# Talking-heads attention with a mixture of experts: the second head of each pair is placed through GpSimd's DMA queue, and the opening is re-ordered

## The chip, the core and the metric

The kernel runs on one core of a Trainium2 chip. A core has five engines that run their own instruction streams: TensorE (PE, with its weight loads shown apart as PEld), VectorE (DVE), ScalarE (ACT), GpSimd (POOL) and SyncE (SP). SP, ACT and POOL can issue DMA transfers, which 16 DMA engines carry out. The metric is the device time of one execution in microseconds (us). Before the change it was 724.6 us, the median of 3 runs (724.17 to 724.93).

## The reference

Twelve heads of attention over 4 batches of 448 tokens, with scores mixed across heads before the softmax (w_pre) and weights mixed across heads after it (w_post); then every token goes to the expert with the highest cosine similarity.

```python
scores = scale * np.matmul(q, k.transpose(0, 1, 3, 2))
scores = np.einsum('bhij,hg->bgij', scores, w_pre)
scores = scores - np.max(scores, axis=-1, keepdims=True)
attn = np.exp(scores)
attn = attn / (np.sum(attn, axis=-1, keepdims=True) + 1e-09)
attn = np.einsum('bhij,hg->bgij', attn, w_post)
x = np.matmul(attn, v)                 # then (4*448, 768)
logits = xn @ en.T / tau               # x and expert_emb normalised
expert_idx = np.argmax(logits, axis=1)
h = np.maximum(x[mask] @ w1[e], 0.0)   # for each of 8 experts
out[mask] = gate_w[mask, None] * (h @ w2[e])
```

## The kernel before, in words

The queries are cut into 16 tiles, four to a batch, of 120 rows (90 in the last tile of a batch; batch 0 begins with its 90-row tile). A tile has six pairs of heads. For each pair PE computes the scores (`emit_qk`, L259) into PSUM; DVE or ACT evicts them to a tile `s` of SBUF (`evict`, L263 to L269; six buffers of `s`); and `place` (L271 to L274) sends each of the two heads of the pair, by a DMA from SBUF to SBUF, into the group layout `g`, where 10 query rows of 12 heads share the partitions. One piece moves 120 (or 90) rows of 448 floats into 10 partitions: 210 or 157.5 KB. There are 96 pairs and so 192 pieces. Three group buffers `gb` serve the tiles in turn; they are called g_133, g_134 and g_135 in the rows of the program order, and tile 0 uses g_135. Their first four partitions are zeroed once.

A tile is then worked off in steps of two blocks of 10 query rows (92 steps in all). For a step, `emit_pre` (L294) multiplies `g` with w_pre on PE, `emit_max` (L302, DVE) and `emit_exp` (L311, ACT) make the softmax numerators `e` and their sums, `emit_r` takes the reciprocal (L319, L321, DVE) and lets POOL scale w_post with it (`wr`, L322), and `emit_post` (L337, L342) multiplies `e` with `wr` on PE. So the chain of a step is pre, max, exp, r, wr, post. In step s the program emits the score matmuls of a later pair, pre of step s+2, wr of step s+1, post of step s, and the placing of a pair as soon as the program order lets its group buffer be free (`held`, `free`). After post come the products with v, the routing, and from step 83 on the loads of the expert weights. The experts' part runs until the end.

The engines run in program order, so what stands ahead in an engine's stream delays what stands behind it. A tile framework adds the semaphore waits. Two of them matter here: a piece waits for the eviction of its `s` (and for the last reader of the group buffer), and every DMA counts on one of a few semaphores taken in turn, eight for the DMAs of SP and ACT together and eight for those of POOL, so that it waits until the DMA that used its semaphore before has landed.

The opening, before the steps begin (L794 to L832), computes 11 pairs (i = 0 to 10). SP loads q and k; POOL loads the small constants and zeroes two of the group buffers (L803); DVE zeroes the third (L799). PE fills its time with matmuls on a tile of ones (`warm`, L808). At i = 9 PE takes up `emit_pre(0)`, which reads the six pairs of tile 0. In the opening the second head of pairs 0 to 5 is sent by ACT, the first head by SP; from pair 6 on both are sent by SP.

Of the kernel before, what the change touches and what calls it, by code (L numbers as in the profile page):

```python
# [33 lines left out]
NPAIR = H // 2  # L34
# [12 lines left out]
def talking_heads_moe(  # L47
# [81 lines left out]
    with tc.manual_schedule():  # L129
# [36 lines left out]
        def embed():  # L166

            em = x_p.tile([128, DM], F32, tag="xs", name="em")[:E]
            ej = x_p.tile([128, DM], F16, tag="xj", name="ej")[:E]
            es = sm.tile([E, 1], F32, tag="es", name="es", bufs=1)  # L170
            G_.dma_start(out=em, in_=emb)
            G_.dma_start(out=wpre_sb, in_=wpre)
            A.activation(out=ej, in_=em, func=ACTF.Square, accum_out=es)
            A.activation(out=wpre_sb, in_=wpre_sb, func=ACTF.Copy, scale=0.125)
            yield
            G_.dma_start(out=rtau, in_=tau.to_broadcast([128, 1]))
            G_.dma_start(out=id_sb, in_=ident)
            G_.dma_start(out=valid_sb, in_=valid)
            G_.dma_start(out=tokid_sb, in_=tokid)
            G_.dma_start(out=tri_sb, in_=tri)  # L180
            yield
            V.tensor_scalar(out=ioE_b, in0=ioE, scalar1=-float(E), scalar2=None, op0=ALU.add)
            yield
            en_n = yield from newton_norm(sm, es, 1, "n1")
            V.tensor_scalar(out=en_n, in0=en_n, scalar1=1e-6, scalar2=None, op0=ALU.add)
            yield
            V.reciprocal(out=en_n, in_=en_n)
            yield
            G_.tensor_scalar(out=em, in0=em, scalar1=en_n[:, 0:1], scalar2=None, op0=ALU.mult)
            G_.tensor_copy(out=ien[:, :, :128], in_=id_sb.unsqueeze(1).to_broadcast([128, KD, 128]))  # L190
            for _ in range(5):
                yield
            p = ps_x.tile([128, 512], F32, tag="x", name="p_e")
            for kk in range(KD):
                T.transpose(p[:, kk * E:(kk + 1) * E], em[:, kk * 128:(kk + 1) * 128], id_sb[:E, :E])
            yield
            V.tensor_copy(out=ien[:, :, 128:], in_=p[:, :KD * E].rearrange("p (k e) -> p k e", e=E))
            V.reciprocal(out=rtau, in_=rtau)
            yield
            V.tensor_scalar(out=tie, in0=rtau, scalar1=-1.0, scalar2=None, op0=ALU.mult)  # L200
            yield
            V.tensor_tensor(out=tie, in0=tie, in1=rtau, op=ALU.max)
            yield
            V.tensor_scalar(out=tie, in0=tie, scalar1=2.0 ** -23, scalar2=None, op0=ALU.mult)
            V.tensor_tensor(out=tv, in0=tokid_sb, in1=valid_sb, op=ALU.mult)
            yield
            V.tensor_scalar(out=ioE_v, in0=ioE_b.unsqueeze(1).to_broadcast([128, NTL, E]), scalar1=-1.0, scalar2=None,
                            op0=ALU.add)
            yield
            V.tensor_tensor(out=ioE_v, in0=ioE_v, in1=valid_sb.unsqueeze(2).to_broadcast([128, NTL, E]), op=ALU.mult)  # L210
            yield
            V.tensor_scalar(out=ioE_v, in0=ioE_v, scalar1=1.0, scalar2=None, op0=ALU.add)
# [34 lines left out]
        def group(t):  # L247

            return gb[which[t]]

        def emit_qk(i, eng, pre=False):

            t, a = divmod(i, NPAIR)
            n = SZ[t]
            pq = ps_q.tile([128, 2, 512], F32, tag="q", name="p_q") if not pre else None
            p = [pq[:, r] for r in range(2)] if pq is not None else [ps_p.tile([128, 512], F32, tag="p", name="p_q") for _ in range(2)]
            for r in range(2):
                for w in range(2):
                    T.matmul(p[r][64 * w:64 * w + 64, :S], q_sb[t][64 * r:64 * r + 64, a, w, :],  # L259
                             k_sb[t // 4, a][64 * r:64 * r + 64], start=True, stop=True)  # L260

            def evict():
                sb = s_p.tile([128, 2, S], F32, tag="s", name="s")  # L263
                split = pq is None
                for o, i in [(sb[:, r], p[r][:, :S]) for r in range(2)] if split else [(sb, pq[:, :, :S])]:
                    if eng is A:
                        A.activation(out=o, in_=i, func=ACTF.Copy)  # L267
                    else:
                        V.tensor_copy(out=o, in_=i)  # L269

                def place(second=Y):  # L271
                    for r in range(2):
                        h = 4 + 2 * a + r
                        (second if r else Y).dma_start(out=group(t)[h:h + 109:12, :n // 10].rearrange("p c s -> p (c s)"), in_=sb[:n, r])  # L274
                return place
            return evict

# [433 lines left out]
        def bg_at(p, f):  # L711
            bg.setdefault(p, []).append(f)
# [84 lines left out]
        ge = embed()  # L797
        next(ge)
        V.memset(gb[2][:4], 0.0)  # L799
        consts()  # L800
        next(ge)
        for g in gb[:2]:
            G_.memset(g[:4], 0.0)  # L803
        p_w = ps_a.tile([128, 512], F32, tag="a", name="p_w")

        def warm(n):
# [3 lines left out]
        pend = []  # L810
        for i in range(N0):
            if i == 9:
                emit_pre(0, ps_m)
            if i == 10:
                emit_pre(1, ps_q)
            pend.append(emit_qk(i, A if i in (0, 8, 10) else V, i % 2 == 1 or i >= 10))
            if i < 9:
                warm(1)
            if i:
                pend.pop(0)()(A if i <= NPAIR else Y)  # L820
            if i == 8:
                load_q(2)
            if i == 9:
                emit_max(0)
                emit_exp(0)
        pend.pop()()()
        emit_max(1)
        emit_exp(1)
        for a in range(NPAIR):
            bg_at(1 + a, lambda a=a: load_v(0, a))  # L830
        warm(4)
        run(emit_r(0))  # L832
        qk_n = N0
        held = []
        placed = N0
# [6 lines left out]
        for s in range(ns):  # L842
            cr = emit_r(s + 1) if s + 1 < ns else iter(())
            evs = []
            ev = emit_post(s) if s == 0 else None
            want = due(s)
            assert want - qk_n < 3
            if qk_n < want:
                evs.append(emit_qk(qk_n, A))
                qk_n += 1  # L850
            if s + LEAD < ns:
                emit_pre(s + LEAD)
            if evict:
                evict()
            while tops:
                tops.pop(0)()
            next(cr, None)
            if evs:
                held.append(evs.pop()())
            while held and free(placed) <= s:  # L860
                held.pop(0)()
                placed += 1
            if s == ns - 2:
                px.close()
                pools["h"] = ctx.enter_context(tc.tile_pool(name="ps_h", bufs=2, space=PSUM))
                st_a = ffn_tok(first_rows["t"], w1p[0], w2p[0], first_rows["g"], idx_s[:, 0:1])
                steps_of(st_a, 1)
            if s == ns - 1:
                steps_of(st_a, 0)
            evict = ev or emit_post(s)  # L870
            next(cr, None)
            if qk_n < want:
                evs.append(emit_qk(qk_n, A))
                qk_n += 1
            for f in acts.pop(s, ()):
                f()
            if s + LEAD < ns:
                emit_max(s + LEAD)
                emit_exp(s + LEAD)
            if evs:  # L880
                held.append(evs.pop()())
                while held and free(placed) <= s:
                    held.pop(0)()
                    placed += 1
            for f in pes.pop(s, ()):
                f()
            for f in dves.pop(s, ()):
                f()
            for x in avs.pop(s, ()):
                emit_av(*x)  # L890
            for f in bg.pop(s, ()):
                f()
            if 3 <= s < 16:
                for _ in range(5):
                    next(ge, None)
            now[0] = s
            if s == first[NE + 1] + 3:
                gens += [(early(), 2), (gate_value(re, 0, NE, bank, routed_bank), 2)]
            if s == OPEN + 1:
                gens += [(first_x(), 1)]  # L900
            if s == first[NG + 1] + 1:
                gens += [(mid(), 2)]
            for g, n in gens:
                for _ in range(n):
                    next(g, None)
# [349 lines left out]
```

## Time and profile before

| | us |
|---|---|
| median of 3 runs | 724.6 |
| the profiled execution | 720.91 |
| its span on the core | 719.1 |
| PE busy | 684.0 |
| DVE busy | 462.0 |
| ACT busy | 393.4 |
| POOL busy | 117.8 |

Busy time is the time in which an engine executes an instruction; matmuls are pipelined, so a busy PE is not PE at its peak. "PEclk" is the share of the full clock (2.4 GHz) that was granted to PE, 0.50 being 1.2 GHz. "DMA" is the mean busy share of the 16 DMA engines. The releaser behind an arrow is what ended the idle time of an engine; "issue" means that the profile shows nothing that was waited for. SPq, ACTq and POOLq are the instruction queues of engines, where DMA issues appear.

### The profile page before, as it was taken

Reading aid. Unit: us, or ns where it says so; the run is one execution under the profiler, and the core shown is the slowest. Engines: PE = TensorE matmul, PEld = TensorE weight load, DVE = VectorE, ACT = ScalarE, POOL = GpSimd, SP = SyncE. Lnnn points to the kernel's source line nnn. Section 1 sums busy time; section 2 is a strip of 40 time slices with the busy share of each in tenths; the row PEclk is TensorE's granted clock in tenths of the full one; section 3 lists DMA queues with packets and bytes.
Section 4 is the critical chain, followed back from the end, with each engine's and each line's share of the span. In section 5 each row is a group of like instructions: output and inputs, shape, how many; then the busy total and the mean of one; then the engine's idle time right before and its main releaser. Section 6 shows DMA issues by size and latency. Waiting matters only on the chain. (4 is left out here: it accounts for less than half of the span.)

```text
span 719.1 us, 26009 instructions
## 1 busy us (share of the span) xinstructions
PE 684.0 (95%) x11132; PEld 560.5 (78%) x11132; DVE 462.0 (64%) x1069; ACT 393.4 (55%) x774; POOL 117.8 (16%) x179
## 2 busy tenths in 40 slices
PE   8788999999999989999999899999999999999983
PEld 4356767766677767676767689999999999999973
DVE  6476666666657656778657656868665656565661
ACT  2455666667567666666666644535263535453540
POOL 7020110110011101110120212330304040200000
PEclk9899999999999999999999999999999999999997
DMA  7676654776457754565343664776767676665750
GB/s 216 194 215 177 183 155 126 228 203 175 130 152 223 201 159 136 153 207 155 98 157 116 187 229 160 262 230 210 227 208 231 209 245 214 195 215 179 224 205 15
DMA packets 56709, 133.08 MB, mean 185 GB/s; under 512 B 6661, under 2 KB 31509, under 8 KB 56592
## 3 DMA queue, kind: packets, MB, share of 16 engines
q1 hardware_dynamic: 52472, 117.98, 53.2%
q0 software_dynamic: 3520, 12.44, 5.1%
q8 instruction: 89, 1.46, 0.8%
q10 hardware_dynamic: 600, 0.97, 0.4%
q14 instruction: 28, 0.23, 0.1%
HBM read 81.64 MB, written 12.20 MB: 130 GB/s over the span
## 5 line engine op out<-in xcount | busy, mean ns | idle before, releaser
L302 DVE TENSOR_REDUCE mn<-p_p 128x1 f32<-128x448 f32 (+1 forms) x182 | 105.6, 619 | 100.3 <-PE p_p L294 99.7
L580 ACT ACTIVATE wh<-raw_w 128x768 fp32r<-128x768 f32 (+2 forms) x132 | 114.9, 903 | 44.8 <-DMA raw_w<-w 39.4
L267 ACT ACTIVATE s<-p_q 128x896 f32<-128x896 f32 (+1 forms) x89 | 80.8, 908 | 104.3 <-PE p_q L259 94.2
L581 DVE TENSOR_TENSOR wl<-raw_w,wh 128x768 fp32r<-128x768 f32 (+2 forms) x132 | 130.9, 1026 | 9.3 <-ACT wh L580 8.8
L311 ACT ACTIVATE e<-p_p,mn 128x448 f32<-128x448 f32 (+1 forms) x182 | 113.6, 628 | 30.1 <-DVE mn L302 26.0
L337 PEld LDWEIGHTS p_m<-wr,e 64*64 64x64 f32 x4320 | 93.8, 135 | 44.4 <-issue 40.7
L337 PE MATMUL p_m<-wr,e 64*64 64x60 f32 x4320 | 95.9, 220 | 4.2 <-issue 3.2
L354 DVE COPY a<-p_m 128x420 f32<-128x420 f32 (+1 forms) x175 | 94.0, 576 | 8.0 <-PE p_m L342 5.5
L259 PE MATMUL p_q<-k,q 64*64 64x448 f32 x768 | 96.9, 569 | 0.9 <-ACT s L267 0.9
L367 PE MATMUL p_av<-a,v 128*64 128x120 f32 (+1 forms) x1536 | 94.8, 266 | 2.4 <-issue 2.4
L1041 PE MATMUL p_h<-xh,wh 128*128 128x256 f32 x336 | 96.6, 288 | 0.0
L294 PE MATMUL p_p<-g,wpre_sb 64*64 64x448 f32 (+1 forms) x712 | 89.7, 547 | 5.9 <-DMA g<-s 5.5
L1041 PE MATMUL p_h<-xh,wl 128*128 128x256 f32 x336 | 94.8, 282 | 0.0
L1041 PE MATMUL p_h<-xl,wh 128*128 128x256 f32 x336 | 94.5, 281 | 0.0
L322 POOL TENSOR_TENSOR wr<-wpost_sb,r 128x120 f32<-128x120 f32 (+1 forms) x92 | 35.4, 385 | 323.6 <-DVE r L321 259.7
L367 PEld LDWEIGHTS p_av<-a,v 128*64 128x64 f32 x1536 | 74.8, 137 | 11.0 <-issue 5.4
L1059 PE MATMUL p_o<-wh,hh 128*128 128x384 f32 x224 | 75.7, 338 | 0.0
L1059 PE MATMUL p_o<-wl,hh 128*128 128x384 f32 x224 | 74.9, 334 | 0.0
L1059 PE MATMUL p_o<-wh,hl 128*128 128x384 f32 x224 | 74.9, 334 | 0.0
L1043 ACT ACTIVATE hh<-p_h 128x512 fp32r<-128x512 f32 x28 | 16.7, 598 | 99.9 <-PE p_h L1041 70.7
L294 PEld LDWEIGHTS p_p<-g,wpre_sb 64*64 64x64 f32 (+1 forms) x712 | 30.0, 135 | 45.1 <-issue 33.2
L1041 PEld LDWEIGHTS p_h<-xl,wh 128*128 128x128 f32 x336 | 63.6, 189 | 0.0
(209 smaller groups left out, 988.6 us busy)
## 6 DMA issues: line engine op xcount, KB each, us to landing
g<-s SPq DMA_DIRECT2D x144, 210.0 KB
raw_w<-w SPq DMA_DIRECT2D x54, 512.0 KB
raw_w<-w SPq DMA_DIRECT2D x72, 384.0 KB
g<-s SPq DMA_DIRECT2D x42, 157.5 KB
v<-vP SPq DMA_DIRECT2D x24, 256.0 KB
q<-qT SPq DMA_DIRECT2D x15, 384.0 KB
k<-kT SPq DMA_DIRECT2D x24, 224.0 KB
x_tok<-xs SPq DMA_DIRECT2D x12, 360.0 KB
```

The costliest lines, as they stand in the source:

```text
L259: T.matmul(p[r][64 * w:64 * w + 64, :S], q_sb[t][64 * r:64 * r + 64, a, w, :], k_sb[t // 4, a][64 * r:64 * r + 64], start=True, stop=True)
L267: A.activation(out=o, in_=i, func=ACTF.Copy)
L294: T.matmul(p[w][64 * x:64 * x + 64, :S], wpre_sb[64 * w:64 * w + 64 - 4 * w], g[64 * w:64 * w + 64 - 4 * w, m + x if nx == 2 else m], star ...
L302: V.tensor_reduce(out=mn[q, c:c + 1], in_=p[u][q, :S], op=ALU.max, axis=AX.X, negate=True)
L311: A.activation(out=e[q, c], in_=p[u][q, :S], func=ACTF.Exp, bias=mn[q, c:c + 1], accum_out=sums[q, c:c + 1])
L337: T.matmul(pm[x][q[c], u * 210 + jt * 60:u * 210 + jt * 60 + 60], e[q[x], u, jt * 128 + 64 * c:jt * 128 + 64 * c + 64], wr[q[x], u], start ...
L354: V.tensor_copy(out=o, in_=i)
L367: T.matmul(p[64 * r:64 * r + 64], v_sb[t // 4, a][:, jt, r * D:(r + 1) * D], a_sb[t % 2][:, c:c + n], start=jt == 0, stop=jt == 3)
L580: A.activation(out=h[:, c], in_=r[:, c], func=ACTF.Copy)
L581: lo = lambda: eng.tensor_tensor(out=l[:, c], in0=r[:, c], in1=h[:, c].bitcast(F32), op=ALU.subtract)
L1041: T.matmul(p[:, f], lt[:, c], rt_[:, k], start=(k == 0 and i == 0), stop=(k == KD - 1 and i == 2))
L1059: T.matmul(p[:, :384], lt[:, k, c], rt_[:, m], start=(k == 0 and i == 0), stop=(k == KF - 1 and i == 2))
```

## The change

From now on `place` always sends the first head of a pair by SP and the second by POOL, for all 96 pairs. In the opening ACT no longer issues DMAs, pairs are evicted by ACT (even i) and DVE (odd i) in turns, the constants that are not needed at once are loaded in the steps 0 to 2 (one DMA for each advance of the generator `ge`), and the zeroing of the two group buffers on POOL is cut into eight pieces of three columns: two ahead of the opening, three in it, three in the steps 4 to 6. The first reciprocal (`emit_r(0)`) is begun at i = 9 and finished at i = 10 instead of after the opening.

```diff
-            G_.dma_start(out=rtau, in_=tau.to_broadcast([128, 1]))
-            G_.dma_start(out=id_sb, in_=ident)
-            G_.dma_start(out=valid_sb, in_=valid)
-            G_.dma_start(out=tokid_sb, in_=tokid)
-            G_.dma_start(out=tri_sb, in_=tri)
-            yield
+            for o, i in ((id_sb, ident), (rtau, tau.to_broadcast([128, 1])), (valid_sb, valid), (tokid_sb, tokid), (tri_sb, tri)):
+                G_.dma_start(out=o, in_=i)
+                yield
...
-                def place(second=Y):
+                def place():
                     for r in range(2):
                         h = 4 + 2 * a + r
-                        (second if r else Y).dma_start(out=group(t)[h:h + 109:12, :n // 10].rearrange("p c s -> p (c s)"), in_=sb[:n, r])
+                        (G_ if r else Y).dma_start(out=group(t)[h:h + 109:12, :n // 10].rearrange("p c s -> p (c s)"), in_=sb[:n, r])
...
-        next(ge)
-        for g in gb[:2]:
-            G_.memset(g[:4], 0.0)
+        pads = [g[:4, c:c + 3] for g in gb[:2] for c in range(0, 12, 3)]
+        for _ in range(2):
+            G_.memset(pads.pop(0), 0.0)
...
-            pend.append(emit_qk(i, A if i in (0, 8, 10) else V, i % 2 == 1 or i >= 10))
+            pend.append(emit_qk(i, V if i % 2 else A, i % 2 == 1 or i >= 10))
...
-                pend.pop(0)()(A if i <= NPAIR else Y)
+                pend.pop(0)()()
+                if NPAIR < i < 10:
+                    G_.memset(pads.pop(0), 0.0)
             if i == 8:
                 load_q(2)
+            if i == 10:
+                run(r0)
             if i == 9:
                 emit_max(0)
                 emit_exp(0)
+                r0 = emit_r(0)
+                next(r0)
         pend.pop()()()
+        for i, x in enumerate(pads):
+            bg_at(4 + i, lambda x=x: G_.memset(x, 0.0))
...
         warm(4)
-        run(emit_r(0))
...
-            if 3 <= s < 16:
-                for _ in range(5):
+            if s < 16:
+                for _ in range(2 if s < 3 else 5):
                     next(ge, None)
```

POOL's stream in the opening, of the kernel before: constants, then the two whole zeroings, then only the wr of the steps.

```order
L176 DMA rtau<-tau 128x1
L177 DMA id_sb<-ident 128x128
L178 DMA valid_sb<-valid 128x16
L179 DMA tokid_sb<-tokid 128x16
L180 DMA tri_sb<-tri 128x128
L803 MEMSET g_133 4x5376
L803 MEMSET g_134 4x5376
L322 TENSOR_TENSOR wr<-wpost_sb,r 128x120 x4
```

The same place of the changed kernel (line numbers move by up to four; L271 is the piece, L319 the wr):

```order
L800 MEMSET g_133 4x1344 x2
L271 DMA g_135<-s 10x9x448 x6
L271 DMA g_133<-s 10x12x448
L819 MEMSET g_133 4x1344
L271 DMA g_133<-s 10x12x448
L819 MEMSET g_133 4x1344
L271 DMA g_133<-s 10x12x448
L819 MEMSET g_134 4x1344
L271 DMA g_133<-s 10x12x448
L319 TENSOR_TENSOR wr<-wpost_sb,r 128x120
L271 DMA g_133<-s 10x12x448 x2
L319 TENSOR_TENSOR wr<-wpost_sb,r 128x120
```

The six pieces of tile 0 stand ahead of everything else that POOL does after two short zeroings, and each wr now stands behind the piece of the same step.

POOL's stream around the steps 4 to 7, before: nothing stands between the wr but the scaling of the expert embedding (em) and the copy of the identity (ien).

```order
L322 TENSOR_TENSOR wr<-wpost_sb,r 128x120 x4
L322 TENSOR_TENSOR wr<-wpost_sb,r 128x60
L322 TENSOR_TENSOR wr<-wpost_sb,r 128x120 x2
L189 TENSOR_SCALAR em<-em,nwy 8x768
L190 COPY ien<-id_sb 128x6x128
L322 TENSOR_TENSOR wr<-wpost_sb,r 128x120 x38
```

And of the changed kernel:

```order
L271 DMA g_134<-s 10x12x448
L319 TENSOR_TENSOR wr<-wpost_sb,r 128x120
L831 MEMSET g_134 4x1344
L271 DMA g_134<-s 10x12x448
L319 TENSOR_TENSOR wr<-wpost_sb,r 128x120
L831 MEMSET g_134 4x1344
L186 TENSOR_SCALAR em<-em,nwy 8x768
L187 COPY ien<-id_sb 128x6x128
L271 DMA g_134<-s 10x12x448
L319 TENSOR_TENSOR wr<-wpost_sb,r 128x120
L831 MEMSET g_134 4x1344
L319 TENSOR_TENSOR wr<-wpost_sb,r 128x120
```

em and ien keep their place behind the seventh wr; a piece and two zeroings come in around them.

DVE's stream at the end of the opening, before: max of step 0, the eviction of pair 9, max of step 1, then both reciprocals.

```order
L269 COPY s<-p_q 128x448 x2
L302 TENSOR_REDUCE mn<-p_p 128x1 x2
L269 COPY s<-p_q 128x448 x2
L302 TENSOR_REDUCE mn<-p_q 128x1 x2
L319 TENSOR_SCALAR r<-su 128x2
L321 RECIPROCAL r<-r 128x2
L319 TENSOR_SCALAR r<-su 128x2
```

And of the changed kernel:

```order
L266 COPY s<-p_q 128x448 x8
L299 TENSOR_REDUCE mn<-p_p 128x1 x2
L316 TENSOR_SCALAR r<-su 128x2
L266 COPY s<-p_q 128x448 x2
L318 RECIPROCAL r<-r 128x2
L299 TENSOR_REDUCE mn<-p_q 128x1 x2
L316 TENSOR_SCALAR r<-su 128x2
```

The addition of the first reciprocal, which needs the sums of exp(0), has moved ahead of the eviction of pair 9.

## Rows read from the trace of the kernel before

**Rows 1.** Busy time of each engine by stage, clock, DMA share, GB/s.

```profile
80.00:380.00 300.00, 293.60 (x7407) 208.90 (x7399) 201.54 (x564) 201.67 (x467) 33.28 (x89) 1.00 0.56 168
```

**Rows 2.** Waits of PE, first 64 us: total us, times, longest.

```profile
PE p_p L294 <- DMA g<-s: 5.5, 1, 5.5
PE p_m L342 <- issue: 1.8, 1, 1.8
PE p_av L367 <- issue: 1.6, 1, 1.6
```

**Rows 3.** Timeline, 12.5 to 23 us: start, us, engine, instruction, idle before.

```profile
12.59 1.16 DVE L269 COPY s<-p_q 128x448 f32<-128x448 f32 x2 [0.20 <-PE p_q L259]
...
17.18 0.92 ACT L267 ACTIVATE s<-p_q 128x896 f32<-128x896 f32 x1 [10.07 <-DMA g<-s]
...
22.44 1.02 PE L294 MATMUL p_p<-g,wpre_sb 64*64 64x448 f32 x4 [5.48 <-DMA g<-s]
```

**Rows 4.** Stretches of 2 us, columns as in rows 1.

```profile
2.00:4.00 2.00, 2.00 (x12) 2.00 (x11) 2.00 (x1) 0.01 (x1) 1.96 (x6) 1.00 1.01 265
...
14.00:16.00 2.00, 2.00 (x17) 0.83 (x20) 1.32 (x2) 0.00 (x0) 1.26 (x1) 1.00 0.65 197
16.00:18.00 2.00, 0.97 (x10) 0.30 (x2) 0.93 (x2) 0.82 (x1) 0.00 (x0) 1.00 0.67 186
...
26.00:28.00 2.00, 2.00 (x16) 0.60 (x10) 1.97 (x5) 0.86 (x4) 0.00 (x0) 1.00 0.66 176
...
44.00:46.00 2.00, 1.82 (x22) 0.82 (x18) 1.83 (x11) 2.00 (x5) 0.00 (x0) 1.00 1.03 249
```

**Rows 5.** Waits of SP's queue, 7 to 17 us.

```profile
SPq L274 <- DMA g<-s: 2.2, 3, 1.1
...
SPq L274 <- DMA q<-qT: 1.6, 1, 1.6
```

**Rows 6.** POOL's groups, whole span: busy us, mean ns, idle before.

```profile
L594 POOL DMA_INDIRECT xg<-x_tok,idx_g x16 | 18.2, 1135 | 8.6 <-ACT hh L646 4.0 <-issue 4.0 <-PE p_t L614 0.3
...
L803 POOL MEMSET g<- 4x5376 f32 x2 | 9.1, 4567 | 0.0
...
L178 POOL DMA_DIRECT2D valid_sb<-valid x1 | 0.6, 592 | 0.0
```

**Rows 7.** Timeline, 0 to 42 us: DVE's zeroing, a POOL issue, the first eviction.

```profile
1.77 3.42 DVE L799 MEMSET g<- 4x4032 f32 x1 [0.78 <-issue]
2.01 0.65 POOL L172 DMA_DIRECT2D wpre_sb<-wpre  x1
...
6.21 0.90 ACT L267 ACTIVATE s<-p_q 128x896 f32<-128x896 f32 x1
```

**Rows 8.** Timeline, 20 to 34 us: the end of the opening.

```profile
25.68 1.16 DVE L269 COPY s<-p_q 128x448 f32<-128x448 f32 x2 [0.28 <-PE p_q L259]
26.04 0.20 ACT L311 ACTIVATION_READ_ACCUMULATOR e<-p_p,mn 128x1 f32 x1
26.36 1.50 PE L259 MATMUL p_q<-k,q 64*64 64x448 f32 x8
...
28.26 0.39 POOL L322 TENSOR_TENSOR wr<-wpost_sb,r 128x120 f32<-128x120 f32 x1 [13.00 <-DVE r L321]
```

**Rows 9.** Timeline, 33.3 to 36.4 us: eviction of step 1, post of step 2.

```profile
33.48 0.91 ACT L267 ACTIVATE s<-p_q 128x896 f32<-128x896 f32 x1
...
36.26 0.26 PE L337 MATMUL p_m<-wr,e 64*64 64x60 f32 x1
```

**Rows 10.** Timeline, 100 to 108 us: eviction of one step, post of the next.

```profile
103.73 0.92 ACT L267 ACTIVATE s<-p_q 128x896 f32<-128x896 f32 x1 [0.76 <-PE p_q L259]
...
107.77 0.34 PE L337 MATMUL p_m<-wr,e 64*64 64x60 f32 x10
```

**Rows 11.** Chosen stretches, columns as in rows 1.

```profile
22.40:25.40 3.00, 2.96 (x16) 1.16 (x20) 1.16 (x2) 0.50 (x1) 0.00 (x0) 0.50 0.73 193
...
49.30:52.70 3.40, 3.40 (x26) 1.60 (x29) 0.00 (x0) 0.80 (x1) 1.62 (x3) 0.51 0.77 217
```

## Prediction

> **What bounds the kernel now.** I read the table by stages first, then PE's waits, then the opening's timeline, then the DMA share in short stretches, and last the rows at which POOL, DVE and ACT meet. Between 80 and 380 us PE is busy for 293.6 of 300 us at the full clock [rows 1]; POOL does 33 us of work there, and no wait on a piece of `g` shows. Whatever a faster placing brings is therefore not to be had in the loop but ahead of it. PE's waits say where: one wait of 5.5 us, in `emit_pre(0)`, for a DMA into `g`; behind it two of 1.8 and 1.6 us for which the profile names nothing ("issue") [rows 2]. All other named waits of PE in 64 us are small.
>
> The timeline shows the long one. Pair 5, the last pair of tile 0, is evicted by 13.75 us (12.59 + 1.16), but PE goes on only at 22.44, after 5.48 idle, when its pieces are there [rows 3]: 8.7 us from the eviction to use. The pieces come at a pace. The eviction of pair 8, on ACT, begins at 17.18, when the pieces of pair 2 have left its buffer (there are six of `s`); those of pair 5 are there at 22.44. That is three pairs in 5.26 us, 1.75 us a pair, slower than PE computes them.
>
> What sets that pace? In the stretches in which little but pieces moves, the 16 DMA engines are busy for 0.65, 0.67 and 0.66 of the time, while they reach 1.01 and 1.03 with loads of q, k and v in flight [rows 4]. A share that stays flat while work queues up looks like about ten engines (0.65 x 16 = 10.4) that are never idle and six that get nothing. SP's waits agree with a full pipe: 3.8 us of the 10 us from 7 to 17 it waits for earlier DMAs to land (2.2 for pieces, 1.6 for a load of q) before it may issue the next [rows 5].
>
> **The change part by part.** The sum is made against the profiled execution (span 719.1, run 720.91 us); it is a difference, which I carry to the median of 724.6, 3.7 us above that execution.
>
> *The second head by POOL, in the opening.* The six second pieces of tile 0 leave ACT's queue for POOL's; SP's six stay. The bytes are the same. If POOL's pieces go to the same ten engines, the pace stays and the gain is nothing; if PE found all pieces there when it is done at 16.97 us (22.44 - 5.48), the whole 5.48 would go. I take an even spread of POOL's half over all 16: the ten then carry 1/2 + 1/2 x 10/16 = 13/16 of what they did, and 3/16 of the stretch in which mostly pieces move, 12 to 22.44 us, is 2.0 us. That is a gain of 2.0, nearer to the lower end, since SP's half remains on the ten. That SP no longer waits for landings adds nothing I would count, as it waits in front of a pipe that is full already; it can't make it later.
>
> A rule of the Trainium skill bears on this (DMA: Bandwidth & Descriptors, "Why a DMA increments its semaphore by 16 and not by 1"): a transfer runs on the largest number of engines up to 16 that divides the slowest dimension of both its sides, the lowest-numbered ones when SP or ACT issue it, while GpSimd's queue takes either all 16 or that many from a start that moves on. With 120 rows on one side and 10 on the other this makes ten, and the flat 0.65 agrees; where POOL's pieces go no trace of this case shows. By the rule the gain would be the same 2.0.
>
> *The constants.* Five loads of POOL (145 KB: two of 64, two of 8, one of 0.5) leave the first 6 us for the steps 0 to 2. At the 265 GB/s of the early loads [rows 4] they took 0.5 us of the pipe in front of the pieces: gain 0.5, between 0 and 0.55. Issued later they cost POOL 0.6 each [rows 6], two to a step.
>
> *The zeroing in pieces.* Eight of 1.1 us, a quarter of the 4.57 of a whole one [rows 6]. The two ahead of the first piece take the place of five loads of 0.6, and so are done before pair 0 is evicted at 7.1 (6.21 + 0.90) [rows 7]. Nothing on the path.
>
> *Evictions in turns.* DVE took 1.16 for a pair and stood idle for PE before it [rows 3]; ACT takes 0.90 [rows 7]. Both keep up with PE, which has to compute the pairs anyway: zero.
>
> *The first reciprocal, begun earlier.* This one costs. DVE now adds to the sums of exp(0) before it evicts pair 9. The sums are there at 26.24 (26.04 + 0.20), the eviction began at 25.68 [rows 8]. So it slips to some 26.4, by 0.7 us. PE's next matmuls (pair 10) started at 26.36, when the first half of that eviction was done; they, the four `warm` and post(0) behind them slip by the same 0.7. The wr(0) that was to come earlier doesn't: on POOL the piece of pair 9 now stands ahead of it and waits for the later eviction, and with 0.6 for that issue wr(0) is done about when it was, 28.65. Cost 0.7, between 0 (if the added time falls into another wait) and 0.8.
>
> *POOL in the loop.* 96 issues come in ahead of the wr. The trace has no piece issued by POOL; its loads of 128 rows took 0.59 and 0.65 us to issue, its indirect ones 1.14 on average [rows 6, 7]. I take 0.6, since a piece has 120 rows and no index. The wr of a step then waits for the eviction, the issue and itself. In the loop: eviction done at 104.65, issue to 105.25, wr to 105.7, and post needs it at 107.77 [rows 10]: 2 us to spare (1.5 at 1.14). Early, where steps are short: eviction done at 34.39, issue and wr to 35.4, post at 36.26 [rows 9]: 0.9 to spare (0.3 at 1.14). So the 58 us of issues hide behind pre, post and the products with v; cover is gone at an issue of about 1.4 us.
>
> *The clock.* PE ran at 0.50 for 22.4 to 25.4 us, 2.96 busy [rows 11], after it had stood since 17. If it resumes earlier the low stretch may end earlier (up to 1.5 back) or cover one more group (0.9 lost). I count 0.
>
> Sum: -2.0 - 0.5 + 0.7 = -1.8: span 717.3, median 722.8.
>
> **The rivals.**
>
> *N, no change.* POOL's pieces run on the same ten engines, or tile 1's pieces, which now queue earlier on POOL, take the room. For it: the pipe is full whoever issues. Against: six engines idle. Then 724.6 - 0.5 + 0.7 = 724.8.
>
> *S, slower: wr late behind the piece.* If POOL's issue takes 2.0 instead of 0.6, wr(2) is done at 34.39 + 2.0 + 0.39 = 36.8, 0.5 after post(2) wanted it; with two constants a step POOL needs 1.2 + 2.0 + 0.4 = 3.6 us where 2.8 lie between the start of the eviction and that post. Some 0.6 in each of five steps makes 3.0; the sixth piece of tile 0 leaves at 7.1 + 12 = 19.1, so the gain of 2.0 is gone too. 724.6 + 3.0 + 0.7 - 0.5 = 727.8. It decides from 1.4 us an issue. Against: the plain loads' 0.59 and 0.65 [rows 6, 7]. The Trainium skill speaks for it (SBUF — State Buffer, "SBUF: two separate sides"): some DVE copies lock GpSimd out of the port over which it writes descriptors. Here POOL issued wpre in 0.65 us while DVE zeroed [rows 7], so this trace doesn't bear it out, and DVE's work in the loop reads PSUM.
>
> *C, more than the opening.* The "issue" waits of 1.6 and 1.8 us [rows 2] go with the fuller spread, and the low clock behind the first (49.3 to 52.7 us, 3.4 busy at 0.51, so 1.7 lost) [rows 11] as well: 5.1 more, 717.7. For it: the DMA share was at 1.03 shortly before the first [rows 4]. Against: no wait on data is named, and the same bytes still move.
>
> **How the numbers follow.** The forecast has 0.48, with a range of its own of 721.0 to 724.6; N 0.22, S 0.12, C 0.18 in full or in part. The range for 8 in 10 runs from 719.0, which leaves out the full C, to 726.5, which takes in N and a mild S. A measurement here tells 0.2% (1.45 us) from no change. Faster (under 723.15): two thirds and more of the forecast's cases (0.36) and C: 0.54. Slower (over 726.05): S and a little of the rest, 0.14. The same: 0.32.
>
> **What would show it.** Right: PE's wait for `g` near 3 us instead of 5.5; a DMA share above 0.65 between 12 and 20 us; POOL's pieces issued in 0.6; the eviction of pair 9 behind exp(0); no wait of PE for wr. Wrong: the wait still over 5 us with a share of 0.65 (N), POOL's pieces at over 1.4 us and PE waiting for wr (S), or PE's gaps near 48 and 61 us gone (C).

## The result: slower by 1.2%

The changed kernel takes 735.5 us (median of 18 runs, 727.1 to 746.6) against 724.8 us of the kernel before in the same series (718.6 to 735.6). The ratio is 1.0122, with a 95% interval of 1.0086 to 1.0159; like every ratio below it leaves disturbed runs out, so it is a little smaller than that of the medians. The forecast was 722.8 us, at most 726.5. The profiled execution took 731.8 us, with a span of 730.0.

**The opening.** PE's waits from 0 to 64 us after the change (tile and line, what it waited for: total, times, longest), which answer to [rows 2]:

```profile
PE p_p L291 <- DMA g<-s: 6.5, 1, 6.5
PE p_av L364 <- issue: 2.8, 1, 2.8
...
PE p_q L256 <- issue: 0.8, 1, 0.8
```

The wait for `g` has grown from 5.5 to 6.5 us instead of shrinking to 3, and the wait without a name at the products with v from 1.6 to 2.8. From the timeline of the same stretch (start, duration, engine, line, operation, and in brackets the idle time before), which answers to [rows 3] and [rows 8]:

```profile
16.71 0.58 POOL L271 DMA_DIRECT2D g<-s  x1
...
23.23 1.77 PE L291 MATMUL p_p<-g,wpre_sb 64*64 64x448 f32 x8 [6.51 <-DMA g<-s]
...
27.05 0.17 DVE L316 TENSOR_SCALAR r<-su 128x2 f32<-128x2 f32 x1 [0.88 <-ACT e L308]
27.23 1.15 DVE L266 COPY s<-p_q 128x448 f32<-128x448 f32 x2
27.91 0.28 PEld L256 LDWEIGHTS p_q<-k,q 64*64 64x64 f32 x4 [1.39 <-DVE s L266]
```

GpSimd issues a piece in 0.58 us, as predicted, but pre(0) starts at 23.23 instead of 22.44. The order on DVE costs what was said: the add comes first, the eviction of pair 9 follows at 27.23, and from pre(0) to the products of pair 10 it is 4.68 us (27.91 - 23.23) instead of 3.92 (26.36 - 22.44).

The DMA engines from 14 to 22 us, before and then after (stretch, length, busy time of PE, PEld, DVE, ACT and POOL, PE's clock, DMA share, GB/s):

```profile
14.00:22.00 8.00, 2.97 (x22) 1.13 (x22) 2.25 (x3) 0.92 (x1) 1.26 (x1) 0.79 0.69 210
```

```profile
14.00:22.00 8.00, 2.72 (x21) 1.00 (x20) 1.16 (x2) 1.59 (x2) 5.65 (x7) 0.96 0.81 186
```

The share rose, as the forecast wanted to see, and the bytes fell. A share that counts packets in progress can rise as well when packets wait for one another.

**The loop.** GpSimd's two groups from 0 to 380 us (count, busy time, mean ns, idle time before):

```profile
L271 POOL DMA_DIRECT2D g<-s x96 | 58.9, 613 | 239.5 <-ACT s L264 179.7 <-ACT xT L376 31.0 <-PE p_m L339 9.0
L319 POOL TENSOR_TENSOR wr<-wpost_sb,r 128x120 f32<-128x120 f32 (+1 forms) x88 | 34.7, 394 | 19.2 <-DVE r L318 17.3 <-DVE r L316 0.4
```

96 issues of 0.61 us, 59 us in all, just as worked out, and PE waits nowhere for `wr`. Yet the loop is slower. The stretch from 80 to 380 us, and PE's longest waits in it, to be held against [rows 1]:

```profile
80.00:380.00 300.00, 289.57 (x7306) 206.03 (x7302) 200.23 (x549) 198.40 (x458) 78.65 (x161) 1.00 0.64 166
```

```profile
PE p_m L334 <- issue: 5.2, 4, 1.9
PE p_m L339 <- issue: 1.8, 1, 1.8
PE p_x L382 <- issue: 1.1, 1, 1.1
```

PE is busy for 289.6 us instead of 293.6; POOL's busy time goes from 33 to 79 us, and the DMA share from 0.56 to 0.64 for no more bytes. PE loses the time in few, single stalls, each put down to "issue", that is, to nothing that the profile names. The spans of the two profiled executions differ by 10.9 us (730.0 and 719.1). Of that, 7.4 us stand at the start of the last `wr` of the loop (392.6 against 385.2), and 3.5 arise behind it, in the experts' part, in which no piece moves; this part lasts 331 to 340 us in the 16 profiles of this case, so one profile's total is no exact measure of the loop.

**What these stalls are.** One of them in the timeline of PE after, and the queue rows of the DMA view for 204.7 to 206.0 us (packets, MB, share of 16 engines):

```profile
205.00 0.28 PE L339 MATMUL p_m<-wr,e 64*64 64x30 f32 x8
207.17 0.57 PE L334 MATMUL p_m<-wr,e 64*64 64x60 f32 x24 [1.89 <-issue]
```

```profile
q1 hardware_dynamic: 66, 0.11, 35.1%
q0 software_dynamic: 33, 0.08, 20.9%
q8 instruction: 1, 0.02, 5.8%
```

In this piece of 1.3 us lies one packet of the instruction queue; the pieces before it (203.5 to 204.6) and behind it (206.0 to 207.1) have none. It takes 1.2 us (5.8% of 16 x 1.3), lands at 205.9, and PE goes on 1.25 us later. Over a whole run this queue moves 89 packets and 1.46 MB, so 16 KB each: by its name code, fetched while the program runs. PE's stream has some 22,500 instructions in the profile (matmuls, weight loads and those of its sequencer); 256 to a packet make 88 blocks.

In the 15 profiles of this case in which ACT issues no piece in the loop there are 89 stalls of PE over 0.5 us that lie between 40 and 380 us (those for the routing's products and for the first expert left out). Of these 87 end 1.2 to 1.8 us, in the middle 1.45, after a packet of that queue has landed; a moment picked at random in the kernel before lies so with a chance of 12%. The same 87 stand in PE's stream at places that differ by multiples of 256 instructions (to within two), in all 15 kernels. The other two, one in e11 and one in e13, stand elsewhere, and the profile puts them down to `wr`. So "issue" here reads: PE has run to the end of a block of code, and the next block came late. It came late because its packet started late, not because the packet was slow: from 80 to 380 us such a packet is in progress for 1.1 to 1.2 us on average in each of the 15 profiles. It starts, on average, 0.9 to 1.3 us after PE has entered the block before (1.3 is the kernel before) when the loop's pieces are on the hardware queues, 1.3 to 1.4 us after it when all second heads are on GpSimd's, and 1.7 in e13. What the packet waits for before it starts no view shows. The two stalls of [rows 2] are of this kind as well.

### The profile page after: what moved, and what is told of

It is laid out like the page before. It is cut to its first block, busy times and chain, and to the rows that moved or that the text cites. A ratio compares the mean times of both kernels' runs of the same rounds, so it can differ in the third digit from the quotient of the medians.

```text
span 730.0 us, 26142 instructions
## 1 busy us (share of the span) xinstructions
PE 687.2 (94%) x11132; PEld 562.9 (77%) x11132; DVE 462.7 (63%) x1066; ACT 396.1 (54%) x777; POOL 178.4 (24%) x281
## 3 DMA queue, kind: packets, MB, share of 16 engines
q8 instruction: 89, 1.46, 0.8%
## 5 line engine op out<-in xcount | busy, mean ns | idle before, releaser
L264 ACT ACTIVATE s<-p_q 128x896 f32<-128x896 f32 (+1 forms) x92 | 83.5, 909 | 107.9 <-PE p_q L256 104.4
L271 POOL DMA_DIRECT2D g<-s x96 | 58.9, 613 | 239.5 <-ACT s L264 179.7
L291 PE MATMUL p_p<-g,wpre_sb 64*64 64x448 f32 (+1 forms) x712 | 91.7, 544 | 6.7 <-DMA g<-s 6.5
L684 POOL DMA_INDIRECT out<-o,idx_s x17 | 22.8, 1340 | 217.9 <-DVE o L1065 168.7
```

The costliest lines, as they stand in the source:

```text
L291: T.matmul(p[w][64 * x:64 * x + 64, :S], wpre_sb[64 * w:64 * w + 64 - 4 * w], g[64 * w:64 * w + 64 - 4 * w, m + x if nx == 2 else m], star ...
```

## The experiments

Theories at the start. Q: the pieces on GpSimd's queue cost, in the opening and in the loop. O: the other edits cost. Later the question was what about that queue: two queues as such (D), the pieces that it carries, or their meeting with the loads (P). All times are medians; ratios are to the kernel before, run in between on the same chip.

**e1, the changed kernel with the pieces back on the hardware queues.**

```
-  (G_ if r else Y).dma_start(out=group(t)[h:h + 109:12, ...
+  ((A if i0 < NPAIR else Y) if r else Y).dma_start(out=group(t)[h:h + 109:12, ...     # i0: the pair
```

> The changed kernel with one part undone: the second head of a pair goes by ACT's queue for tile 0 and by SP's for the rest, as before; constants in the loop, zeroing in pieces, evictions in turns and the early first reciprocal stay. Q (the pieces on GpSimd's queue cost the time): about 725.5 us, that is before plus the 0.7 of the first reciprocal, at most 727; PE's wait for g in the opening back to 5.0 to 5.6 us; DMA share at 80 to 380 us back to 0.56. O (the other edits cost it): 733 to 736.

718.9 us, ratio 0.9968 (0.9934 to 1.0001). PE's wait for `g`, and 80 to 380 us:

```profile
PE p_p L292 <- DMA g<-s: 2.4, 1, 2.4
```

```profile
80.00:380.00 300.00, 295.40 (x7483) 210.66 (x7475) 203.57 (x571) 203.63 (x471) 33.76 (x90) 1.00 0.57 168
```

O falls: the other edits together gain about 0.3%, at the edge of the error. The whole loss, 1.5% between the two ratios, is the queue. And the wait for `g` is 2.4 us, not the 5 that Q expected: one of the other edits shortens it.

**e2, the kernel before with GpSimd's queue in the loop alone.**

```
+  ((G_ if i0 >= N0 else second) if r else Y).dma_start(...     # N0 = 11
```

> The kernel before with the second head on GpSimd's queue only from pair 11 on (the 85 pairs of the loop); its opening is untouched. Q, if the loss is spread over the loop: 724.8 plus about 6 (the part of the lag that grew after step 2 in the profile after, 7.4 - 1.5), some 730 to 733; PE's wait for g in the opening stays at 5.5. If the loss were made in the opening: under 726.5.

736.3 us, ratio 1.0167 (1.0098 to 1.0236): 12 us (7 to 17 by the interval), so the loss of the changed kernel is reached by the loop alone. From 80 to 380 us, a stretch behind a stall of 2.9 us at 222.3, and that stall among the waits:

```profile
80.00:380.00 300.00, 289.26 (x7222) 204.30 (x7218) 197.01 (x543) 195.41 (x452) 77.42 (x158) 0.99 0.62 163
...
226.60:229.90 3.30, 3.30 (x32) 1.39 (x36) 0.13 (x1) 1.29 (x2) 0.38 (x1) 0.50 0.54 120
```

```profile
PE p_x L386 <- issue: 2.9, 1, 2.9
```

The same 289 us of PE as in the changed kernel. The second row shows that this stall cost twice: behind it PE ran for 3.3 us at a clock of 0.50.

**e3, the kernel before with GpSimd's queue in the opening alone.**

```
+  ((G_ if i0 < N0 else second) if r else Y).dma_start(...
```

> The kernel before with the second head on GpSimd's queue only for pairs 0 to 10, the opening; the loop as before. Q: the wait for g in the opening becomes 6 to 6.6 us instead of 5.5, and the time rises by 0.8 to 1.5, to 725.6 to 726.3. What the prediction held (half the pieces on all 16 engines): wait near 3.5 us, time 722.8.

722.9 us, ratio 1.0004 (0.9973 to 1.0035). It doesn't tell what it was meant to, since another wait took over: PE waited

```profile
PE p_q L260 <- DVE s L270: 6.5, 1, 6.5
```

GpSimd's zeroing in two wholes lasts until 15.3 us here, so the first six pieces leave late and hold the buffers of `s`. In the profile pre(0) comes at 24.61 us, 2.2 later than in the kernel before, though the times don't show it. e8 repeats the test with the zeroing in pieces.

**e4, the changed kernel with the second head on ACT's queue throughout.**

```
+  (A if r else Y).dma_start(...
```

> The changed kernel with the second head on ACT's queue for all pairs: like GpSimd's a second queue beside SP's, but one whose pieces look like SP's. Q, if it is how GpSimd's queue moves a piece that costs: 725 to 728 (ACT pays about 0.05 to 0.1 us an issue, 96 of them), DMA share at 80 to 380 us about 0.56. If any second queue beside SP's costs (pieces that overtake the loads): 732 to 736 and a share of 0.6 or more.

752.8 us, ratio 1.0416 (1.0369 to 1.0464), against both expectations. The stretch from 80 to 380 us and PE's longest wait between 40 and 390:

```profile
80.00:380.00 300.00, 278.68 (x6758) 196.83 (x6757) 190.11 (x517) 184.38 (x422) 28.41 (x80) 1.00 0.51 153
```

```profile
PE p_x L382 <- ACT xT L376: 17.5, 24, 1.5
```

The issues on ACT's queue (duration in ns: least, middle, greatest; first and last start in us):

```profile
L271 ACTq DMA_DIRECT2D g<-s x96: 785/786/1427, 7.5 to 383.4; - x96
```

Another mechanism: a piece on ACT's queue leaves only when ACT's own eviction is done, and its issue then keeps ACT for 0.79 us, not for the 0.05 to 0.1 that was expected; ACT stands idle for 0.86 to 0.9 us each time, and what stands behind it on ACT is late, with PE among those who wait for it. The DMA share per byte (0.51 for 153 GB/s) is that of e1 (0.57 for 168), not that of the changed kernel (0.64 for 166). So the share rises with the pieces on GpSimd's queue, not with those on ACT's; of code loads e4 tells little, as PE ran slower.

**e5 and e6, GpSimd's queue for six tiles each.** Both start from e1. In e5 they are the tiles whose pieces are placed in the steps in which SP loads the k or v of the next batch, in e6 those in between; 36 pairs in both.

```
e5  +  ((G_ if t in (3, 6, 7, 10, 11, 14) else A if t == 0 else Y) if r else Y).dma_start(...
e6  +  ((G_ if t in (4, 5, 8, 9, 12, 13) else A if t == 0 else Y) if r else Y).dma_start(...
```

> The kernel of e1 with the second heads of six tiles (3, 6, 7, 10, 11, 14: 36 pairs) on GpSimd's queue; their pieces are placed in the steps in which SP also loads the k or v of the next batch. P (the price is paid where pieces meet loads, and code for PE comes late): most of the 16.6 us between e1 and the changed kernel, less the 3 of the opening: 10 to 13 us over e1's 718.9, some 729 to 732. C (each piece by GpSimd costs the same wherever it stands): 36 of 85 of 13.6, 5.8 us: 724.7.

> As e5, but for the six tiles whose pieces are placed between the loads of k and v (4, 5, 8, 9, 12, 13: 36 pairs as well). P: 0 to 3 us over e1's 718.9, 719 to 722. C: 724.7, the same as e5.

727.7 us, ratio 1.0108 (1.0044 to 1.0172), and 724.1 us, ratio 1.0024 (0.9987 to 1.0061). Over e1 that is 1.4% (10 us) and 0.6% (4 us). 80 to 380 us in e5, then in e6:

```profile
80.00:380.00 300.00, 291.43 (x7353) 207.32 (x7356) 200.20 (x554) 199.74 (x462) 52.24 (x119) 1.00 0.60 165
```

```profile
80.00:380.00 300.00, 293.53 (x7397) 209.27 (x7390) 202.30 (x561) 201.38 (x467) 55.75 (x125) 1.00 0.60 167
```

As many pieces cost over twice as much where they meet the loads (fewer bytes even: two of e5's tiles have 90 rows). That is P in part only: e6 is not free, and the two intervals overlap at their ends. The expectations started from 16.6 us between medians of different series; by the ratios it is 1.5%, 11 us. Of e2's 1.7%, 36 of 85 pairs would have 0.7%, which e6 about shows, and e5 shows twice that.

**e7, the loads on GpSimd's queue and the pieces on SP's.** From e1:

```
-  Y.dma_start(out=k_sb[b, a], in_=kT[b, :, a])
+  (G_ if b else Y).dma_start(out=k_sb[b, a], in_=kT[b, :, a])      # v alike; q from tile 3 on
```

> The kernel of e1 (all pieces by SP, tile 0's second heads by ACT) with the loads of q, k and v of the loop (48 + 13 loads, 15 MB) on GpSimd's queue: about as many bytes on that queue beside SP's pieces as the changed kernel has, but in long rows from DRAM. D (two queues that together have up to 16 transfers in flight crowd PE's code loads, whatever they carry): 728 or more. Q (the pieces' short rows by GpSimd's queue cost engine time): within 2 us of e1, 717 to 721, DMA share at 80 to 380 us 0.56 to 0.58.

720.8 us, ratio 1.0001 (0.9960 to 1.0042), within the error of e1. By the edit 36 loads of k and v and 13 of q moved, 14 MB.

```profile
80.00:380.00 300.00, 295.79 (x7472) 210.76 (x7466) 204.38 (x574) 204.24 (x474) 57.01 (x134) 1.00 0.54 167
```

PE is as busy as in e1. D falls: 14 MB on a second queue, with GpSimd issuing, do no harm beyond the error when they are loads. It matters what GpSimd's queue carries. The length of the rows is not what tells the two apart, though the expectation says so: a row of k has 448 floats, 1792 B, like a row of a piece. The pieces go from SBUF to SBUF and into 10 partitions, the loads from DRAM into 128.

**e8, GpSimd's queue in the changed kernel's opening alone.**

```
+  ((G_ if i0 < N0 else Y) if r else Y).dma_start(...
```

> The changed kernel with GpSimd's queue for the second heads of pairs 0 to 10 alone; the loop's go by SP. Against e1 this leaves the opening's part by itself, with the zeroing in pieces that e3 lacked. Q: PE's wait for g near 6 us against e1's 2.4, pre(0) at about 23 against 20.4 us; time 721 to 722, 2 to 3 over e1. What the prediction held: pre(0) earlier than e1's, time at or under 718.9.

722.2 us, ratio 1.0017 (0.9978 to 1.0056). PE's wait for `g`, and 14 to 22 us:

```profile
PE p_p L292 <- DMA g<-s: 4.8, 1, 4.8
```

```profile
14.00:22.00 8.00, 3.16 (x26) 1.31 (x30) 1.16 (x2) 1.83 (x2) 5.85 (x7) 0.95 0.90 205
```

The wait is twice e1's 2.4, pre(0) at 21.9 instead of 20.4 us, and the time about 0.5% over e1, which is the size of the error. The share is 0.90, the highest of all, with fewer bytes than e1 moves at 0.67 (213 GB/s). The predicted gain in the opening is a loss in the profile.

**e9, e1 with the first reciprocal as before.**

```
-  if i == 10: run(r0)            # and its start behind emit_exp(0)
+  run(emit_r(0))                 # behind warm(4)
```

> The kernel of e1 with the first reciprocal back behind the four warm-up products, as before. R (beginning it earlier costs what the prediction said): PE's wait of 0.82 us for the eviction of pair 9 goes, from pre(0) to the products of pair 10 it is 3.9 us again instead of 4.7, time 0.7 under e1, 718.2. If the wr that is now later holds PE up: 718.9 or more, with a wait for wr at post(0).

719.4 us, ratio 0.9931 (0.9891 to 0.9971), the best of all. From pre(0) to the products of pair 10 it is 3.97 us (24.43 - 20.46) against e1's 4.68, so the 0.7 is there in the profile; in the times it is less than the error (0.9931 against 0.9968), and so "best" is not told from e1.

**e10, the kernel before with the evictions in turns and nothing else.**

```
-  pend.append(emit_qk(i, A if i in (0, 8, 10) else V, i % 2 == 1 or i >= 10))
+  pend.append(emit_qk(i, V if i % 2 else A, i % 2 == 1 or i >= 10))
```

> The kernel before with one edit, the evictions of the first eleven pairs on ACT and DVE in turns; constants, zeroing, first reciprocal and queues as before. V (the turns make e1's shorter wait for g): wait for g 2 to 3.5 us, time 720 to 721. K (the late constants and the zeroing in pieces make it): wait 4.2 to 5.5 us as in the kernel before and in e2, time 722.5 to 724.

721.3 us, ratio 0.9989 (0.9949 to 1.0029). PE's wait for `g`, and 14 to 22 us:

```profile
PE p_p L294 <- DMA g<-s: 2.8, 1, 2.8
```

```profile
14.00:22.00 8.00, 4.36 (x33) 1.84 (x37) 1.16 (x2) 1.83 (x2) 1.25 (x1) 0.94 0.69 234
```

V, by the profile; the times alone don't show a gain. The turns alone bring the wait down to 2.8 us and pre(0) to 20.7. Part of the shorter wait is that PE itself is ready later (17.92 instead of 16.97), so pre(0) is the better measure; and e2, with the opening of the kernel before, has it at 21.1 after a wait of 4.2. The late constants and the zeroing in pieces, which e10 lacks, are worth little. The second row goes against how I had read the DMA share: at the same 0.69 as in the kernel before the engines moved 234 instead of 210 GB/s.

**e11, GpSimd's pieces in two halves of the columns.**

```
+  for c in (slice(0, 224), slice(224, S)):
+      G_.dma_start(out=group(t)[h:h + 109:12, :n // 10, c], in_=sb[:n, r, c])
```

> The changed kernel with each of GpSimd's pieces cut into two transfers of half the columns: as many bytes, twice the rows (896 instead of 1792 B), twice the issues (0.6 us each). B (big packets in turn with the others are what crowds PE's code loads): fewer and shorter stalls, 725 to 732. S (each short row costs the engines, however big): DMA share at 80 to 380 us 0.70 or more instead of 0.64, time 740 or more.

739.8 us, ratio 1.0197 (1.0120 to 1.0273); 80 to 380 us:

```profile
80.00:380.00 300.00, 289.27 (x7167) 204.97 (x7167) 199.19 (x540) 193.96 (x445) 121.26 (x233) 0.99 0.65 167
```

Neither. The time isn't below the changed kernel's, as B wanted, and the share stays at 0.65, not at 0.70 as S wanted. The edit changed less than it was meant to: in the changed kernel GpSimd's queue moves a piece in packets of 5376 B, three rows, and in e11 most of its bytes go in packets of 4480 B, five half rows (packets of the traces, 80 to 380 us). So of the rows' and the packets' size this leaves the question open, and big packets on GpSimd's queue stay a rival that no run tested.

**e12, e7 with the first reciprocal as before.** The edits of e7 and e9 together.

> The kernel of e7 (pieces by SP and ACT, the loop's loads by GpSimd) with the first reciprocal as before: a version that may beat both kernels. If moving the loads takes stalls out of the loop (e7's profile shows one of 2.6 at 45 us and none over 0.5 from there to 320): 717 to 719. If e7's profile was chance: 720, as e7, less 0.7.

719.6 us, ratio 0.9963 (0.9930 to 0.9996): faster than the kernel before, and not to be told from e9. Moving the loads gains nothing on top.

**e13, both heads of the loop's pairs on GpSimd's queue.** From e9:

```
+  (G_ if i0 >= N0 else A if r and i0 < NPAIR else Y).dma_start(...
```

> The kernel of e9 with both heads of the loop's pairs (pair 11 on) on GpSimd's queue; SP carries the loads and the stores alone. Q (each piece on GpSimd's queue costs, by itself): twice what the second heads cost in e2 (12 us over the kernel before), so some 20 to 25 over e9's 719.4: 739 to 744. W (it is the second and the first head's pieces of a pair running side by side from two queues that crowds): at most e2's 12, 722 to 731.

748.9 us, ratio 1.0322 (1.0258 to 1.0386). 80 to 380 us, and PE's waits from 80 to 390:

```profile
80.00:380.00 300.00, 278.84 (x6793) 196.65 (x6787) 191.55 (x519) 184.81 (x423) 116.53 (x225) 0.98 0.64 154
```

```profile
PE p_m L335 <- issue: 8.7, 5, 3.8
PE p_m L335 <- POOL wr L320: 3.7, 2, 3.1
PE p_m L340 <- issue: 3.4, 2, 1.8
```

W falls: with none of the loop's pieces on SP's queue the stalls for code grow, and now `wr` does come late as well (3.7 us), the price of two issues a step. Outside this stretch PE also waits once for 5.6 us (35 to 41 us), for an eviction whose buffer of `s` the pieces still hold.

**e14, the loads and the second heads on GpSimd's queue.** From e12, with GpSimd for the second heads from pair 11 on.

> The kernel of e12 (the loop's loads of q, k and v by GpSimd) with the second heads of the loop's pairs on GpSimd's queue too; SP is left with the first heads and the stores. Q: as e2, 12 us over e12's 719.6, some 730 to 733, with stalls of PE in the loop that nothing is named for. W2 (the harm is that SP's loads run ahead beside GpSimd's pieces; in one queue they would follow each other): 719 to 724. If GpSimd now holds wr up (pieces and loads wait in one queue): over 735, with PE's waits on wr.

722.0 us, ratio 1.0033 (0.9993 to 1.0072).

```profile
80.00:380.00 300.00, 290.20 (x7312) 206.53 (x7308) 200.18 (x550) 198.35 (x459) 100.47 (x201) 1.00 0.62 164
```

Over e12 it is 0.7%, 5 us, where the same pieces cost 12 in e2. By the times it helps that the loads follow the pieces in one queue instead of running beside them; the one profile, with 290 us of PE, still has the stalls. The two don't agree well enough to call W2 shown.

## Why the prediction was wrong

*POOL in the loop: the step that failed.* "So the 58 us of issues hide behind pre, post and the products with v." Every number of that step came true (0.61 us an issue, no wait for `wr`), and the step fell all the same, because it asked only when GpSimd and `wr` would be late. It didn't ask what 85 transfers moved to another queue do to those that nobody in the program waits for. PE's code comes over the same engines, and with the pieces on GpSimd's queue more of its blocks came late: PE's busy time from 80 to 380 us is 293.6 to 295.9 in the eight profiles with the loop's pieces on SP's queue (293.6 is the kernel before, 295.4 is e1), 291.4 and 293.5 with GpSimd's for some tiles (e5, e6), 289.3 to 290.2 with it for all second heads (the changed kernel, e2, e11, e14). The loss in the loop is about 12 us (e2).

*The opening: sign wrong.* A gain of 2.0 was forecast from an even spread over 16 engines; in the changed kernel's own opening the queue costs about 2 us. pre(0) comes at 23.23 us in the changed kernel and at 21.90 in e8, which has the same opening, against 19.8 to 22.0, 20.6 on average, in the eight profiles with that opening and its second heads on the hardware queues (e1, e5 to e7, e9, e12 to e14). So one profile of an opening differs from the next by up to 2 us, and only the mean tells. The premise was that a flat DMA share of 0.65 means ten engines that are never idle. e10 moved a ninth more bytes at the same share, and e8 fewer at 0.90, so the share tells neither how full the engines are nor how many get work. Where GpSimd's pieces went no view shows, so the spread itself stays open.

*Evictions in turns: costed at zero, worth about 1 us.* "Both keep up with PE" looked at the engines' busy time. In the kernel before, DVE evicts seven pairs in a row; with ACT taking every other one pre(0) comes at 20.74 us (e10) instead of 22.44 and 21.10 (the kernel before and e2). Why is open in part: the eviction of pair 5 ends at 13.80 instead of 13.75, and yet its two pieces are issued at 14.43 and 14.66 instead of 15.53 and 15.71; 0.3 of that is a start of the whole run that was earlier by chance. In the changed kernel the queue took this gain back (pre(0) at 23.23).

*Constants, zeroing, first reciprocal, clock.* The constants were put at 0.5; between e10 (20.74) and the mean of the eight (20.6) they and the zeroing leave less than one profile differs from the next. That the zeroing is off the path held, for a reason not given: in two wholes it would have held the first pieces up (e3). The reciprocal was put at 0.7 and shows 0.71 (e1 against e9). For the clock 0 was taken; in the changed kernel the low stretch of the opening covers 4.9 us of busy PE (23.2 to 28.1 us, at 0.50) instead of 3.0, which at half speed is an estimated 0.9 us lost, the worse of the two cases that the prediction named. In the loop the stall of 2.9 us in e2 is followed by 3.3 us at half speed.

*The rivals.* S had the right sign by the wrong way: its point of decision, 1.4 us an issue, was never near. What was held against it stands. The rule of the Trainium skill that spoke for it (SBUF — State Buffer, "SBUF: two separate sides") warns of some DVE copies that keep GpSimd from writing its descriptors; 0.61 us an issue over 96 issues, with DVE at work, shows no such hold-up here. C looked at the right rows, the "issue" waits, and had their direction wrong; N didn't happen. What no rival held is that a queue can cost through traffic that isn't the program's own.

*What is shown and what isn't.* Shown: the loss comes with the pieces on GpSimd's queue (e1, e2), not with that queue as such (e7), and grows with their number (e13); from 80 to 380 us PE loses it in front of late code. By the times it is larger where the pieces meet loads (e5, e6), just beyond the error. Not shown: why a block's packet starts later beside these pieces. Three things are on record. First, by the queue rows of e9 and of the changed kernel the pieces' packets were in progress for 71 us per MB on GpSimd's queue, and the hardware queues lost 44 us with every MB that left them (queue: packets, MB, share of 16 engines' span; spans 714.8 and 730.0 us):

```profile
q1 hardware_dynamic: 52472, 117.98, 53.6%
q0 software_dynamic: 3520, 12.44, 5.1%
...
q10 hardware_dynamic: 600, 0.97, 0.4%
```

```profile
q1 hardware_dynamic: 41312, 99.59, 45.6%
q0 software_dynamic: 10816, 31.83, 16.8%
```

(0.168 x 730.0 - 0.051 x 714.8) x 16 over 19.4 MB is 71, and (0.540 x 714.8 - 0.456 x 730.0) x 16 over the same is 44. Second, the 44 is too low as the price of a piece there, since what stays on SP's queue got slower: packet by packet, from 80 to 380 us, those of 1792 B on SP's queue, most of them rows of pieces, take 53 us per MB in the kernel before and 59 in the changed one, where GpSimd's packets of 5376 B take 69. Third, the size of the packet isn't all: loads of k, which GpSimd's queue also moves in packets of 5376 B, take 0.21 us each in e7, pieces 0.31 in the changed kernel (middle values). Since a share can pass 1 [rows 4], such a time holds waiting too, and doesn't tell a slow packet from a crowded one.

## What to carry to other kernels

When transfers move to another queue, look beyond their issue time and their waiters: the engines are shared with transfers that no instruction waits for, PE's code first of all, and a loop in which PE is 98% busy has little room for a late block. Read "issue" gaps of PE against the instruction queue before calling them nameless, and judge a DMA change by bytes per time and by PE's busy time in the stretch, not by the busy share of the engines. The version to keep is e9: the evictions in turns, constants and zeroing as in the change, the first reciprocal and all queues as before, 0.7% faster than the kernel before (0.3 to 1.1% by the interval; e1 and e12 are not told from it).

## What the hardware showed that I had not expected

- PE resumed 1.2 to 1.8 us after a 16 KB code block had landed, 87 of 89 times, and always at the end of a block of 256 instructions; in the changed kernel such stalls are 8.7 of the 10.4 us that PE loses from 80 to 380 us (5.2 + 1.8 + 1.1 + 0.6).
- 14 MB of loads cost nothing beyond the error on GpSimd's queue (e7), up to 19 MB of pieces 1.2 to 1.7% (the changed kernel, e2), though the rows of k are as short as those of the pieces, 1792 B.
- A piece issued on ACT's queue behind ACT's own eviction keeps ACT idle for about 0.9 us each time, 0.79 of it the issue itself: with 96 of them the kernel is 4.2% slower (e4).
- The DMA engines' busy share ran from 0.67 to 0.90 in the same 8 us of the opening while the bytes stayed between 186 and 234 GB/s, without a relation between the two.
